# Attention, first expansion and gate folding in an order planned over all engines

## The chip, the cores and the metric

The kernel runs on one core of a Trainium2 chip. The metric is device time in microseconds (us) of one execution. TensorE (PE) multiplies, VectorE (DVE), ScalarE (ACT) and GpSimd (POOL) do the rest, and SyncE (SP) issues the transfers. Each engine runs its own instructions strictly in program order and waits on semaphores for the others.

## What is computed

Inputs are q, k, v of 4 batches, 12 heads, 448 positions and 64 dimensions; a dense expansion 768 to 2048 to 768; and eight experts.

```python
scores = np.where(mask, -1e9, scale * np.matmul(q, k.transpose(0, 1, 3, 2)))   # causal
attn = softmax(scores)
x = np.matmul(attn, v)                       # 1792 tokens x 768
h = x @ w_in                                 # 768 -> 2048, the "first expansion"
g = np.where(h > 0, h, np.exp(np.minimum(h, 0)) - 1)
x = g @ w_out                                # 2048 -> 768
logits = x @ w_gate                          # 8 experts, 224 tokens each, by rank
out = relu(x[chosen] @ w1[e]) @ w2[e]
```

This study is about the lines down to g and about the "gate folding", which computes w_out @ w_gate so that logits come from g directly. The weights w_in and w_out arrive as 8-byte numbers and are converted to 4-byte ones on VectorE.

## The kernel before

**Attention** works on 24 pairs of heads (6 pairs, NP, make one batch). `front(n)` multiplies the scores of pair n, seven tiles of 448 down to 64 columns (tile `sc` in PSUM; for the first six pairs alternately `sc` and `h`, two buffers each). For each tile VectorE masks and takes the row maximum into `s` (L209), ScalarE takes the exponential (L213), VectorE the reciprocals of the sums for three and then four tiles (L220, L221), and GpSimd scales the rows (L228). `back(n)` transposes the scaled tiles on TensorE (tile `tp`, two buffers, L249), copies them to `pt` (L252) and multiplies with v (the second product, tile `pv`, L262). Its result is split into a high part `xh` (ScalarE, L268) and a rest `xl` (VectorE, L269). `att(n)` interleaves `back(n)` with `front(n+1)`.

**The first expansion**, `gemm1(b)`, has 16 feature chunks (MT) for a batch, each the sum over six pairs (KT); one piece (m, c) is three matmuls of 448 columns (L377 to L379, tile `h`, two buffers). For each chunk `split_in` splits a weight tile into `wh` (ScalarE, L361) and `wl` (L362), by a fixed rule on GpSimd for batches 0 to 2 and on VectorE for batch 3. In batch 0 each chunk's weights are first converted by `conv`: a clamp `cv` (L169), a high part `cq` (L174) and a join (L178), all on VectorE, from a staged load `st` of 768 KB.

**The gate folding**, `fold()`, does the same conversion for 16 tiles of w_out, writes each back (`wo_d`), transposes it (L323, six transposes into `tp`), and multiplies with w_gate (L313) and `sel` (L319).

**Order.** `Sched` keeps a model time `now`, advanced by what TensorE's instructions cost. Work of other engines is put in a heap by `after(d, fn)` and written into the program d nanoseconds of model time later; `need(tok)` writes everything up to that work first. Which engine takes an operation is fixed in the code. `drive` takes the next TensorE step from the stream that is furthest behind its weight:

```python
sch.drive((seq(*[att_l(n) for n in range(-1, 6)]), 54000))
for b in range(3):
    g = [(seq(*[att_l(n) for n in range(6 * b + 6, 6 * b + 12)]), 45000), (gemm1(b), 57600)]
```

So the first seven `att_l` run the attention of batch 0 alone, and then `gemm1(b)` runs beside the attention of batch b + 1. The folding starts late in b = 0 and runs through b = 1. `gemm1(3)` follows with the first products of the second expansion, then `gemm2`, the routing and the experts.

## Time and profile before

| | us |
|---|---|
| median of 3 runs | 1049.47 (1047.4 to 1051.67) |
| the profiled execution, its own time | 1051.09 |
| its span, first to last instruction | 1049.3 |
| TensorE busy | 1012.6, 97% of the span |
| VectorE busy | 638.1, 61% |
| ScalarE busy | 469.1, 45% |
| GpSimd busy | 234.4, 22% |

TensorE's busy time is a union of matmuls whose ends are modelled, and a matmul counts as busy from its issue, also while it waits for the one in front. So 97% does not mean that 97% of the span was useful; how much was is found from the distance between starts of matmuls that follow each other without a wait.

### The profile page before, as it was taken

The page shows a single profiled execution, that of the slowest core. Times are in us where ns is not written, and L with a number is a line of the kernel's source. Part 1 is how long each engine was busy: PE and PEld are TensorE (multiplying, and loading weights), DVE is VectorE, ACT ScalarE, POOL GpSimd, SP SyncE. Part 2 cuts the span into 40 slices and gives each one's busy share as a digit, 9 for nine tenths or more (in the row PEclk, how much of TensorE's full clock was granted, in tenths as well). Part 3 has the DMA queues.
Part 4 walks back from the last instruction along what each step waited for, and adds up shares of the span by engine and source line. Part 5 has one row for each costly group of instructions (what it writes and reads, how often), then busy time and mean ns, then how long its engine had stood idle before and what let it go on. Part 6 is the DMA issues. An engine that isn't in the chain of part 4 may idle for free.

```text
span 1049.3 us, 17726 instructions
## 1 busy us (share of the span) xinstructions
PE 1012.6 (97%) x6615; PEld 874.3 (83%) x6615; DVE 638.1 (61%) x1531; ACT 469.1 (45%) x1024; POOL 234.4 (22%) x311
## 2 busy tenths in 40 slices
PE   8799999989999999999999999999999999999997
PEld 4568777667777777888898988999999999999997
DVE  5778866767744333445766566656446766667761
ACT  5565556445455555454212111111245666556651
POOL 4456554334344444000000000000030111101110
PEclk9999999999999999999999999999999999999999
DMA  7545644655622110765333323222166787676800
GB/s 182 141 123 182 208 165 141 224 191 190 210 68 88 63 45 27 256 202 162 106 106 116 121 91 102 72 76 71 67 203 210 242 253 225 210 243 221 261 30 27
DMA packets 110857, 155.32 MB, mean 148 GB/s; under 512 B 29617, under 2 KB 82353, under 8 KB 110770
## 3 DMA queue, kind: packets, MB, share of 16 engines
q1 hardware_dynamic: 108210, 143.17, 43.4%
q0 software_dynamic: 2560, 11.01, 3.5%
q8 instruction: 52, 0.85, 0.3%
q14 instruction: 35, 0.29, 0.1%
HBM read 122.17 MB, written 31.98 MB: 147 GB/s over the span
## 4 chain that ended last, share of the span: by engine, by line
PE 81%; DVE 8%; ACT 3%; DMA 3%; issue 2%; POOL 2%; SPq 0%; POOLq 0%; DVEq 0%; ACTq 0%
PE h L633 9%; PE tp L633 8%; PE h L938 8%; PE h L377 7%; PE sc L990 6%; PE h L379 6%; PE h L378 6%; PE sc L204 5%; PE pv L262 4%; PE h L935 4%; PE tp L249 3%; PE pv L990 3%; PE lg L990 3%; PE lg L772 2%; DMA st<-in_moe_w_out_dram 1%
## 5 line engine op out<-in xcount | busy, mean ns | idle before, releaser
L377 PE MATMUL h<-xh,wh 128*128 128x448 f32 x384 | 170.8, 445 | 0.0
L509 DVE TENSOR_TENSOR wl<-wr,wh 128x768 fp32r<-128x768 f32 x144 | 135.4, 952 | 17.5 <-ACT wh L508 17.2
L379 PE MATMUL h<-xh,wl 128*128 128x448 f32 x384 | 140.9, 367 | 0.0
L378 PE MATMUL h<-xl,wh 128*128 128x448 f32 x384 | 140.7, 366 | 0.0
L213 ACT ACTIVATE s<-s,sm 128x448 f32<-128x448 f32 (+6 forms) x168 | 84.9, 506 | 105.5 <-DVE sm L209 104.8
L508 ACT CAST wh<-wr 128x768 fp32r<-128x768 f32 x144 | 118.2, 829 | 29.9 <-PE lg L990 23.4
L938 PE MATMUL h<-xt,wh 128*128 128x448 f32 x384 | 119.2, 374 | 0.0
L228 POOL TENSOR_SCALAR s<-s,sm 128x448 f32<-128x448 f32 (+6 forms) x168 | 90.2, 554 | 116.2 <-DVE sm L221 105.1
L362 POOL TENSOR_TENSOR wl<-wr,wh 128x768 fp32r<-128x768 f32 x48 | 90.2, 1880 | 106.4 <-ACT wh L361 100.7
L643 ACT COPY x<-h 128x384 f32<-128x384 f32 x14 | 6.7, 480 | 230.5 <-PE h L633 230.5
L204 PE MATMUL sc<-kT,qz 128*128 128x192 f32 (+6 forms) x300 | 92.5, 400 | 5.4 <-DVE sm L209 4.3
L209 DVE CUSTOM_DVE_ANT_0 s<-sc,mask 128x448 f32<-128x448 f32 (+6 forms) x150 | 62.1, 420 | 57.1 <-PE sc L204 51.0
L394 DVE SCALAR_TENSOR_TENSOR g<-e,h 128x448 f32<-128x448 f32 x64 | 39.6, 619 | 88.2 <-ACT e L391 88.1
L935 PE MATMUL h<-xt,wl 128*128 128x224 f32 x384 | 92.2, 267 | 0.0
L377 PEld LDWEIGHTS h<-xh,wh 128*128 128x128 f32 x384 | 72.5, 189 | 17.6 <-issue 9.7
L633 PE MATMUL h<-wh,gh 128*128 128x384 f32 x224 | 81.2, 363 | 0.0
L378 PEld LDWEIGHTS h<-xl,wh 128*128 128x128 f32 x384 | 72.9, 190 | 9.4 <-issue 3.2
L379 PEld LDWEIGHTS h<-xh,wl 128*128 128x128 f32 x384 | 72.4, 188 | 6.7 <-POOL wl L362 0.6
L633 PE MATMUL h<-wl,gh 128*128 128x384 f32 x224 | 77.4, 345 | 0.0
L633 PE MATMUL h<-wh,gl 128*128 128x384 f32 x224 | 76.6, 342 | 0.0
L633 PE MATMUL tp<-wh,gl 128*128 128x384 f32 x224 | 75.4, 336 | 0.0
L633 PE MATMUL tp<-wl,gh 128*128 128x384 f32 x224 | 75.3, 336 | 0.0
(209 smaller groups left out, 2127.7 us busy)
## 6 DMA issues: line engine op xcount, KB each, us to landing
wr<-in_moe_w_dram SPq DMA_DIRECT2D x128, 384.0 KB, 3.8
gT_d<-g SPq DMA_DIRECT2D x64, 224.0 KB, 1.9
gr<-gT_d SPq DMA_DIRECT2D x28, 512.0 KB, 4.0
st<-in_moe_w_in_dram SPq DMA_DIRECT2D x16, 767.6 KB, 4.6
st<-in_moe_w_out_dram SPq DMA_DIRECT2D x16, 767.6 KB, 5.0
wo_d<-wo SPq DMA_DIRECT2D x16, 384.0 KB, 3.2
wr<-wo_d SPq DMA_DIRECT2D x16, 384.0 KB, 3.7
qz<-in_q_dram SPq DMA_DIRECT2D x48, 112.0 KB, 3.3
```

The lines of the kernel that those rows point to most:

```text
L204: PE.matmul(p[:, :w], qT[:, i].rearrange("p a c -> p (a c)"), kT[:, :w], start=True, stop=True)
L228: G.tensor_scalar(s[:, :w], s[:, :w], sm[:, 2, i:i + 1], 1.0, op0=OP.mult, op1=OP.mult)
L362: t = after(800, lambda: (V if b == 3 else G).tensor_sub(wl, WIN[m], wh.bitcast(F32)))
L377: PE.matmul(p[:, :S], wh[:, c], xh, start=(c == 0), stop=False)
L378: PE.matmul(p[:, :S], wh[:, c], xl, start=False, stop=False)
L379: PE.matmul(p[:, :S], wl[:, c], xh, start=False, stop=(c == KT - 1))
L508: A.copy(wh, raw)
L509: return wh, wl, after(gap, lambda: e.tensor_sub(wl, raw, wh.bitcast(F32)))
L633: PE.matmul(p[n][:, :384], st[:, mm], wsel[:, 384 * n:384 * n + 384], start=(m == 0 and first), stop=(m == MT - 1 and st is gl))
L935: PE.matmul(p[:, :CAP], wl[:, c], xt[:, c, :CAP], start=False, stop=stop, skip_group_check=True)
L938: PE.matmul(p[:, :2 * CAP], wh[:, c], xt[:, c], start=(c == 0), stop=(c == KT - 1), skip_group_check=True)
L990: PE.matmul(acc[j][n][:HC, :384], ht[:, m, s, j * HC:(j + 1) * HC], wsel[:, 384 * n:384 * n + 384], start=(m == 0 and first), stop=(m == F ...
```

## The change

`Sched` becomes a list scheduler. `job(cost, deps, fn, prio)` takes a cost for each engine that may do the work; `best` picks, among the jobs whose dependencies have an end in the model, the one that can start first (then by priority), on the engine where it ends first; `pop` books that engine. A stream now yields what its next TensorE step waits for, its cost, and the PSUM buffers that it takes; `drive` takes a step only when the model says that it is ready. Conversions get the lowest priority (3). The split `wl` may go to VectorE or GpSimd (batches 0 to 2), the copies of transposed tiles to ScalarE or VectorE. One pair's `front` may run ahead of `back` by up to two pairs. In the first batch scores use `sc` (two buffers) and `lg` (one), which leaves `h` to the expansion: the first two chunks of `gemm1(0)` take piece (0, c) and (1, c) as soon as pair c is done. The three tiles for v become fixed, with one clearing each instead of 24.

```diff
     def __init__(self):
-        self.now, self.heap, self.n = 0.0, [], 0
+        self.now, self.n, self.jobs, self.free, self.rings = 0.0, 0, [], {}, {}
+
+
+    def job(self, cost, deps, fn, prio=0):
+        self.n += 1
+        tok = Tok()
+        self.jobs.append((prio, self.n, cost, list(deps), fn, tok))
+        return tok
...
+    def ended(self):
+        return Tok(self.now + LAT_PE)
...
+    def best(self):
+        top = None
+        for j in self.jobs:
+            prio, n, cost, deps, fn, tok = j
+            r = self.when(deps)
+            if r is not None:
+                e = min(cost, key=lambda e: max(r, self.free.get(e, 0.0)) + cost[e])
+                z = max(r, self.free.get(e, 0.0)), prio, r, n
+                if top is None or z < top[0]:
+                    top = z, j, e
+        return top
...
+    def pop(self, top):
+        z, j, e = top
+        self.jobs.remove(j)
+        end = z[0] + j[2][e]
+        if e is not None:
+            self.free[e] = end
+        j[5].t = end + (LAT if e is not None else 0.0)
+        j[4](e)
...
-    def drive(self, *gens):
-        st = [[g, 0.0, t] for g, t in gens]
-        while st:
...
+    def drive(self, *streams, until=lambda: False):
+        st = [[[g if isinstance(g, list) else [g, ((), 0.0, ())] for g in (gs if isinstance(gs, tuple) else (gs,))],
...
+        while st and not until():
+            top = self.place(self.now)
+            pick, first, n = None, top and top[0][0], 0
+            for s in st:
+                for g in s[0]:
+                    r = self.ready(g)
+                    if r is None:
+                        continue
+                    if r <= self.now + 60.0:
+                        z, n = s[1] / s[2], n + 1
+                        if pick is None or z < pick[0]:
+                            pick = z, s, g, r
+                        break
+                    first = r if first is None else min(first, r)
+            if pick is None:
+                self.now = max(self.now, first)
+                continue
...
+            self.now = max(self.now, r)
+            self.place(self.now)
+            self.now += g[1][1]
+            s[1] += g[1][1]
...
-                c = next(s[0])
-                s[1] += abs(c)
-                self.tick(max(c, 0))
...
+    def load64(i):
+        if i < 2 * MT:
+            STG[i] = wf.tile([128, DM * 8], U8, name="st")
+            LD[i] = Tok(sch.now + 6500.0)
+            src = w_in[i] if i < MT else w_out[(i - MT) * 128:(i - MT + 1) * 128]
+            SP.dma_start(STG[i][:, :DM * 8 - 3], src.bitcast(U8)[:, 3:])
+
...
+        def join(_):
+            V.scalar_tensor_tensor(dst.bitcast(I32), tl["x"], 5, tl["d"], op0=OP.logical_shift_right, op1=OP.bitwise_or)
+            load64(i + 2)
+
+        t = sch.job({V: 640.0}, [lambda: LD.get(i), lambda: JOIN.get(i - 1)], clamp, 3)
+        t = sch.job({V: 1250.0}, [t], high, 3)
+        JOIN[i] = sch.job({V: 1030.0}, [t], join, 3)
...
+        yield [lambda: DONE.get(n - 2)], 0.0
+        if n + 2 < NB * NP:
+            load_qk(n + 2)
+        if n + 1 < NB * NP:
+            load_v(n + 1)
+        for fn in EARLY.get(n, ()):
+            fn()
         qT, kT = qz[n % 3], KN.pop(n)
         sm = at.tile([128, 3, 8], F32, name="sm", bufs=3)
...
+            nm, nb = ("lg", 1) if n < NP and i in (5, 2) else ("sc", 2)
+            yield [], max(1.68 * w, 222.0), ((nm, nb),)
...
+            def ev(e, p=p, i=ii[0], nb=nb, ni=ni):
+                (V.tensor_copy if e is V else A.copy)(
...
+            w = 128 * nb * ni
+            tk.append(sch.job({A: 0.82 * w + 60, V: 1.04 * w + 90}, [sch.ended()], ev))
...
-            conv_in(m + 2, m + 4)
-        need(WTOK[m])
+            conv_in(m + 2)
         wh = wk.tile([128, KT, 128], F32R, name="wh")
         wl = wk.tile([128, KT, 128], F32R, name="wl")
-        A.copy(wh, WIN[m])
-        t = after(800, lambda: (V if b == 3 else G).tensor_sub(wl, WIN[m], wh.bitcast(F32)))
-        sp[m] = wh, wl, t
+        t1 = sch.job({A: 790.0}, [JOIN[m]], lambda _: A.copy(wh, WIN[m]), 1)
+        t2 = sch.job({V: 930.0} if b == 3 else {V: 930.0, G: 1850.0}, [t1],
+                     lambda e: e.tensor_sub(wl, WIN[m], wh.bitcast(F32)), 1)
+        sp[b, m] = wh, wl, t1, t2
...
-
-        for m in range(MT):
-            wh, wl, tok = sp.pop(m)
-            need(tok)
-            p = ps.tile([128, 512], F32, name="h")
-            for c in range(KT):
-                (t1, xh), (t2, xl) = XH[b * NP + c], XL[b * NP + c]
...
-                yield 567
-                if c == 0:
-                    split_in(b, m + 1)
...
+        P = {}
+        order = [(m, c) for m in range(MT) for c in range(KT)]
+        if b == 0:
+
+            order[:2 * KT] = [(m, c) for c in range(KT) for m in range(2)]
+        for m, c in order:
+            n = b * NP + c
+            yield [lambda: XL[n][0] if n in XL else None, lambda: sp[b, m][3] if (b, m) in sp else None], 609.0, (
+                (("h", 2),) if c == 0 else ())
...
+            split_in(b, m + 2)
...
-    sch.drive((seq(*[att_l(n) for n in range(-1, 6)]), 54000))
-    for b in range(3):
-        g = [(seq(*[att_l(n) for n in range(6 * b + 6, 6 * b + 12)]), 45000), (gemm1(b), 57600)]
-        if b == 0:
-            fd = fold()
-            g.append((seq(wait(85000), one(fd)), 105000))
-        if b == 1:
-            g.append((fd, 18 * 6080))
-        sch.drive(*g)
...
+    EARLY = {1: [lambda: conv_in(0)], 2: [lambda: conv_in(1), lambda: split_in(0, 0)], 3: [lambda: split_in(0, 1)],
+             4: [consts_gate]}
+    stream = lambda g: [g, ((), 0.0, ())]
+    att = stream(seq(*[back(n) for n in range(NB * NP)])), stream(seq(*[front(n) for n in range(NB * NP)]))
+    gem = stream(seq(*[gemm1(b) for b in range(3)]))
+    sch.now = 6000.0
+    sch.drive((att, 1.0e9), (gem, 1.0), until=lambda: NP - 1 in XL)
+    sch.drive((att, 132000), (gem, 182600), (fold(), 1.0e9))
...
-    sch.drive((gemm1(3), 57600), (split_out(), 48000), (logits0(), 45000), (seq(wait(50000), pre()), 51000))
+    sch.drive((gemm1(3), 62000), (split_out(), 48000), (logits0(), 45000), (seq(wait(50000), pre()), 51000))
```

What this makes of the order is shown at three places. The names are those of the code; numbers behind s, qz and vn are buffers.

The first place is VectorE at the end of pair 0's scores, with what each instruction waits for. Before:

```order
L209 ISA s_99,sm<-h,mask 128x128 [waits PE_49]
L209 ISA sm 128x1
L209 ISA s_97,sm<-sc,mask 128x64 [waits PE_49]
L209 ISA sm 128x1
L220 TENSOR_SCALAR sm<-sm 128x3 [waits Activation_49]
L221 RECIPROCAL sm<-sm 128x3 [waits DVE_49]
L209 ISA s_110,sm<-sc,mask 128x448 [waits PE_49]
L209 ISA sm 128x1
```

In the change:

```order
L304 ISA s_99,sm<-sc,mask 128x128 [waits PE_49]
L304 ISA sm 128x1
L261 TENSOR_SCALAR cv<-st 128x768 [waits DMAHW0_49]
L318 TENSOR_SCALAR sm<-sm 128x3 [waits Activation_49]
L319 RECIPROCAL sm<-sm 128x3 [waits DVE_49]
L304 ISA s_97,sm<-sc,mask 128x64 [waits PE_49]
L304 ISA sm 128x1
L304 ISA s_110,sm<-sc,mask 128x448 [waits PE_49]
```

The clamp of the first weight tile, which waits for a transfer, now stands ahead of pair 0's first reciprocals.

The second place is TensorE between the second products of two early pairs (of pairs 0 and 1 before, then of the change):

```order
L204 MATMUL sc<-kT,qz_95 128x192
L204 MATMUL h<-kT,qz_95 128x128
L204 MATMUL sc<-kT,qz_95 128x64
L204 MATMUL sc<-kT,qz_96 128x448
L249 MATMUL tp<-ident,s_110 128x128 x4
L249 MATMUL tp<-ident,s_108 128x128 x3
L249 MATMUL tp<-ident,s_106 128x128 x3
L204 MATMUL h<-kT,qz_96 128x384
L249 MATMUL tp<-ident,s_102 128x2x64 x2
L249 MATMUL tp<-ident,s_104 128x2x64 x2
L249 MATMUL tp<-ident,s_98 128x2x64
L249 MATMUL tp<-ident,s_100 128x2x64
```

```order
L341 MATMUL tp<-ident,s_110 128x128 x4
L341 MATMUL tp<-ident,s_108 128x128 x3
L300 MATMUL sc<-kT,qz_96 128x448
L341 MATMUL tp<-ident,s_106 128x128 x3
L341 MATMUL tp<-ident,s_102 128x2x64 x2
L341 MATMUL tp<-ident,s_104 128x2x64 x2
L300 MATMUL lg<-kT,qz_96 128x384
L341 MATMUL tp<-ident,s_98 128x2x64
L341 MATMUL tp<-ident,s_100 128x2x64
L300 MATMUL sc<-kT,qz_96 128x320
L467 MATMUL h<-xh,wh 128x448
L468 MATMUL h<-xl,wh 128x448
```

The transposes of pair 1 now begin right behind the product of pair 0, since its scores were all written ahead of it, and the first piece of the expansion stands among them.

The third place is VectorE in the middle of the folding. Before:

```order
L169 TENSOR_SCALAR cv<-st 128x768
L209 ISA s_106,sm<-sc,mask 128x320
L209 ISA sm 128x1
L174 ISA cq,dummy<-st,cv 128x768
L174 ISA dummy 128x1
L220 TENSOR_SCALAR sm<-sm 128x3
L221 RECIPROCAL sm<-sm 128x3
L209 ISA s_104,sm<-sc,mask 128x256
L209 ISA sm 128x1
L178 SCALAR_TENSOR_TENSOR wo<-st,cq 128x768
L394 SCALAR_TENSOR_TENSOR g<-e,h 128x448
L325 COPY woT<-tp 128x384
```

In the change:

```order
L361 TENSOR_TENSOR xl<-pv,xh 128x448
L446 TENSOR_TENSOR wl<-wr,wh 128x768
L261 TENSOR_SCALAR cv<-st 128x768
L484 SCALAR_TENSOR_TENSOR g<-e,h 128x448
L419 COPY wp<-tp 128x8
L265 ISA cq,dummy<-st,cv 128x768
L265 ISA dummy 128x1
L268 SCALAR_TENSOR_TENSOR wo<-st,cq 128x768
L304 ISA s_103,sm<-sc,mask 128x256
L304 ISA sm 128x1
L446 TENSOR_TENSOR wl<-wr,wh 128x768
L304 ISA s_101,sm<-sc,mask 128x192
```

The weight rests wl now stand on VectorE between two conversions. Of the 64 wl of the first expansion VectorE does 58 in the change and 16 before, GpSimd 6 and 48. Between the xl of pair 10 and that of pair 14 VectorE has 14 conversions in the change and 11 before. From the 77th matmul of the second expansion on, the order of TensorE is the same as before but for a shift of two routing steps.

## Rows read from the trace of the kernel before

**Rows 1.** Timeline of TensorE beside the expansion: start us, us, what, count.
```profile
150.46 0.36 PE L377 MATMUL h<-xh,wh 128*128 128x448 f32 x1
...
151.07 0.70 PE L204 MATMUL sc<-kT,qz 128*128 128x320 f32 x2
```

**Rows 2.** Timeline of TensorE, first pairs; in brackets idle before and its releaser.
```profile
1.19 4.45 PE L446 MATMUL pv<-warm 128*128 128x512 bf16 x10 [1.19 <-DVE warm L443]
...
12.97 1.11 PE L249 MATMUL tp<-ident,s 128*128 128x128 f32 x7 [0.47 <-POOL s L228]
...
14.75 0.81 PE L204 MATMUL h<-kT,qz 128*128 128x384 f32 x2
15.40 0.82 PE L249 MATMUL tp<-ident,s 128*128 128x128 f32 x6
16.05 0.70 PE L204 MATMUL sc<-kT,qz 128*128 128x320 f32 x2
```

**Rows 3.** The chain that ended last: start us, us, what; second products of pairs 5, 10, 17, 23.
```profile
63.20 1.88 PE pv L262 x16
...
154.05 1.88 PE pv L262 x16
...
310.15 1.88 PE pv L262 x16
...
414.11 1.88 PE pv L262 x16
```

**Rows 4.** Timeline of TensorE in the folding.
```profile
187.67 0.42 PE L313 MATMUL tp<-woT,wg 128*32 128x128 f32 x6
```

**Rows 5.** Stretches: length, busy us of PE, PEld, DVE, ACT, POOL, clock, DMA share, GB/s.
```profile
63.20:154.05 90.85, 87.70 (x482) 70.61 (x483) 71.25 (x175) 52.05 (x133) 50.53 (x54) 1.00 0.53 167
154.05:310.15 156.10, 147.35 (x986) 111.94 (x988) 102.52 (x262) 80.45 (x213) 61.06 (x74) 0.99 0.54 179
310.15:414.11 103.96, 102.16 (x587) 80.76 (x588) 40.47 (x136) 57.90 (x147) 48.31 (x62) 1.00 0.18 57
...
191.90:264.00 72.10, 68.42 (x476) 51.52 (x475) 52.14 (x126) 36.13 (x97) 29.27 (x32) 0.98 0.63 204
```

**Rows 6.** Tile st, loads of the first 14 us: count, ns, first and last start us.
```profile
L152 SPq DMA_DIRECT2D st<-in_moe_w_in_dram x2: 583/584/585, 5.7 to 9.4; - x2
...
DMA to landing us min/median/max: 7.8/7.8/7.8
```

**Rows 7.** Timeline of VectorE, pair 0.
```profile
11.88 0.17 DVE L221 RECIPROCAL sm<-sm 128x3 f32<-128x3 f32 x1
```

**Rows 8.** VectorE groups by form, 0 to 500 us: count, busy us, mean ns, idle before.
```profile
L174 DVE CUSTOM_DVE_ANT_0 cq<-st,cv 128x768 int32<-128x768 int8 x32 | 44.6, 1394 | 0.1
...
L394 DVE SCALAR_TENSOR_TENSOR g<-e,h 128x448 f32<-128x448 f32 x64 | 39.6, 619 | 88.2 <-ACT e L391 88.1
L169 DVE TENSOR_SCALAR cv<-st 128x768 bf16<-128x768 int8 x32 | 21.2, 662 | 10.5 <-DMA st<-in_moe_w_out_dram 10.5
...
L178 DVE SCALAR_TENSOR_TENSOR wo<-st,cq 128x768 int32<-128x768 int32 x16 | 16.8, 1050 | 0.1
...
L362 DVE TENSOR_TENSOR wl<-wr,wh 128x768 fp32r<-128x768 f32 x16 | 15.2, 952 | 0.3
...
L209 DVE CUSTOM_DVE_ANT_0 s<-sc,mask 128x448 f32<-128x448 f32 x24 | 14.8, 616 | 4.3 <-PE sc L204 4.3
...
L209 DVE CUSTOM_DVE_ANT_0 s<-sc,mask 128x64 f32<-128x64 f32 x24 | 5.3, 221 | 4.4 <-PE sc L204 3.8 <-POOL vn L145 0.4
```

**Rows 9.** Tile st, first 60 us: ns min/median/max.
```profile
L174 DVE CUSTOM_DVE_ANT_0 cq<-st,cv x3: 1115/1115/1117, 31.0 to 50.6; 128x768 int32<-128x768 int8 x3
```

**Rows 10.** GpSimd groups by form, 0 to 500 us.
```profile
L362 POOL TENSOR_TENSOR wl<-wr,wh 128x768 fp32r<-128x768 f32 x48 | 90.2, 1880 | 106.4 <-ACT wh L361 100.7 <-PE tp L323 5.4
L228 POOL TENSOR_SCALAR s<-s,sm 128x448 f32<-128x448 f32 x24 | 18.1, 756 | 61.9 <-DVE sm L221 52.9 <-ACT s L213 9.0
```

**Rows 11.** Waits of VectorE, 150 to 300 us: us in total, times, longest.
```profile
DVE cv L169 <- DMA st<-in_moe_w_out_dram: 10.5, 5, 4.4
```

More of the change, by code (lines that the diff above doesn't have):

```diff
@@ L34, with __init__, ring, hold @@
 MASK = -8.0e9
+LAT_PE, LAT = 300.0, 60.0
+class Tok:
+    def __init__(self, t=None):
+        self.t = t
 class Sched:
     def __init__(self):
[L42 to L53 removed]
+        self.now, self.n, self.jobs, self.free, self.rings = 0.0, 0, [], {}, {}
[4 more added lines that the diff above has]
+        return tok
+    def after(self, d, fn):
+        return self.job({None: 0.0}, [Tok(self.now + d)], lambda e: fn())
+    def ended(self):
+        return Tok(self.now + LAT_PE)
+    def ring(self, name, n):
+        r = self.rings.setdefault(name, [])
+        return r[-n] if len(r) >= n else []
+    def hold(self, name, *toks):
+        self.rings.setdefault(name, []).append(list(toks))
+    def when(self, deps):
+        r = 0.0
+        for d in deps:
+            d = d() if callable(d) else d
+            if d is None or d.t is None:
+                return None
+            r = max(r, d.t)
+        return r
+    def best(self):
[17 more added lines that the diff above has]
+        j[4](e)
+    def place(self, t):
+        while True:
+            top = self.best()
+            if top is None or top[0][0] > t:
+                return top
+            self.pop(top)
@@ new lines, in ready @@
+    def ready(self, g):
+        deps, _, rings = g[1]
+        return self.when(list(deps) + [d for n, k in rings for d in self.ring(n, k)])
+    def drive(self, *streams, until=lambda: False):
+        st = [[[g if isinstance(g, list) else [g, ((), 0.0, ())] for g in (gs if isinstance(gs, tuple) else (gs,))],
+               0.0, w] for gs, w in streams]
+        while st and not until():
[15 more added lines that the diff above has]
+                continue
+            _, s, g, r = pick
+            self.now = max(self.now, r)
+            self.place(self.now)
+            self.now += g[1][1]
+            s[1] += g[1][1]
+            try:
+                c = next(g[0])
+                g[1] = (c + ((),))[:3] if isinstance(c, tuple) else ((), 0.0, ())
+                if not isinstance(c, tuple):
+                    s[1] += abs(c)
+                    self.now += max(c, 0)
+                    if c < 0 and n == 1 and first is not None:
+                        self.now = max(self.now, first)
@@ L128, in body @@
     PB = [[at.tile([128, 128 * ((i + 2) // 2)], F32, name=f"s{i}{k}", bufs=1) for k in range(2)] for i in range(NQ)]
-    KN, VN, WIN, STG = {}, {}, {}, {}
+    VT = [at.tile([128, 4, 2, D], F32, name=f"vn{i}", bufs=1) for i in range(3)]
+    KN, WIN = {}, {}
     def load_qk(n):
@@ new lines, in gemm1 @@
+        order = [(m, c) for m in range(MT) for c in range(KT)]
[5 more added lines that the diff above has]
+                (("h", 2),) if c == 0 else ())
+            GPOS[0] = max(GPOS[0], b * MT + m)
+            if c == 0:
+                P[m] = ps.tile([128, 512], F32, name="h")
+            p = P[m]
+            wh, wl = sp[b, m][:2]
+            xh, xl = XH[n][1], XL[n][1]
+            PE.matmul(p[:, :S], wh[:, c], xh, start=(c == 0), stop=False)
+            PE.matmul(p[:, :S], wh[:, c], xl, start=False, stop=False)
+            PE.matmul(p[:, :S], wl[:, c], xh, start=False, stop=(c == KT - 1))
+            if c == 1 and b == NB - 1:
+                load_wo(m)
+            if c == 3 and LATE:
+                yield from late()
+            if c < KT - 1:
+                continue
+            split_in(b, m + 2)
@@ L403, in gemm1 @@
                 gs = []
+        G1[b] = sch.ended()
     LATE, L_TOK = [], []
@@ L449, in body @@
     load_v(0)
-    load64_in(0)
+    load64(0)
+    load64(1)
     for t in qz:
```

272 lines of the change are left out of this document (99 added, 173 removed).

## The prediction

> **What bounds the kernel now.** I read the chain of waits first. It runs almost wholly over TensorE, so time is won only where TensorE has nothing to do or waits. Its busy share can't show that, so I price its work by the distance of starts. One piece of the expansion, three matmuls, holds it 0.61 us: the first of three starts at 150.46 and the next other work at 151.07 [rows 1]. A score tile of 384 columns holds it 0.65 us (14.75 to 15.40), and six transposes as long (15.40 to 16.05) [rows 2]; so a pair's seven tiles with 1792 columns cost 3.0 us and its 16 transposes 1.74. The second product takes 1.88 us [rows 3]. A pair is 6.6 us of TensorE. One folding tile is six transposes, 0.65, and small products of some 0.4 [rows 4]; a group of logits is taken as 1 us, half a second product.
>
> Then I set the starts of second products in the chain [rows 3] against the work that the program has between them, counted in its order.
>
> - To 63.20 us (pair 5): 4.4 us of warming matmuls [rows 2] and 6 pairs and 4 score tiles, less the product that follows, 40.1: 44.5 of work, 18.7 lost.
> - 63.20 to 154.05 (pairs 6 to 10): 5 pairs 33.1, 83 pieces 50.6: 83.7 of 90.9, 7.2 lost.
> - 154.05 to 310.15 (pairs 11 to 17, with the folding): 7 pairs 46.3, 106 pieces 64.7, 16 folding tiles 17, three logit groups 3: 131 of 156.1, 25 lost.
> - 310.15 to 414.11: 6 pairs less four score tiles 37.3, 92 pieces 56.1, four logit groups 4: 97.4 of 104.0, 6.6 lost. Behind it nothing worth a term.
>
> So some 57 us are lost before 414 us, and the reader is to see where: in the head and in the folding. VectorE is the busiest helper: 71.25 of 90.85 us beside batch 0's expansion, 102.52 of 156.10 in the folding, 52.14 of 72.10 in its densest part, but only 40.47 of 103.96 behind it [rows 5].
>
> **The change, part by part.** TensorE's work is the same, so each term is a part of these losses. The terms go against the profiled execution, 1051.09 us (its span is 1049.3); the median of before is 1.6 lower.
>
> *Head.* Two things pull apart. Against: the clamp of the first weights now stands on VectorE ahead of pair 0's reciprocals. Its load is issued at 5.7 us and lands 7.8 us later [rows 6], at 13.5; the planner assumed 6.5 us. The reciprocals ended at 12.05 [rows 7] and the transposes came 0.9 later, at 12.97 [rows 2]. In the change: 13.5, clamp 0.7 [rows 8], reciprocals 0.4, then 0.9: 15.5, 2.5 us later. TensorE meanwhile does two more score tiles of pair 1 (1.2 us), so 1.3 are lost. Behind the first transposes come the others, each pair of them waiting for a copy out of the two tp buffers on a ScalarE and a VectorE that have pair 1's tiles to do as well: 5.5 us by my walk through both orders, then the product, which ends at 22.9. Whether the second weight load, now issued right behind the first, delays it, no row shows: at most by its own length, 768 KB at 203 GB/s [rows 5], 3.8 us, and the lower bound below takes that in. The Trainium skill (DMA: Bandwidth & Descriptors, Queues, rings and completion order) says that on each DMA engine descriptors are consumed in ring order; by that there is no such delay.
> For: pair 1's scores are written by then, its transposes follow at once, and pieces of the expansion fill gaps. From 22.9 I go pair by pair with the larger of TensorE's and VectorE's work. Pairs 1, 3, 4, 5 are TensorE's: 6.2, 6.7, 8.7, 7.0 with small waits. Pair 2 is VectorE's: up to its xl the change has 4 clamps, 4 high parts, 3 joins and 2 wl where before has 2, 1, 1 and 0, 8.6 us more by [rows 8], the high part at the 1.115 that it took this early [rows 9]; less what backlog pair 1 leaves room for, it takes 10.4. The sum, 39.0, puts the start of pair 5's product at 60.0 us instead of 63.2, with 3.4 us more work done (five pieces and a small tile): 6.6 gained. I take 5, since a walk by hand leaves out small waits; bounds 2 and 8.
>
> *Pairs 6 to 10.* VectorE's work is close to TensorE's here in both orders (it ran 78% of the time and 7.2 us were lost). I take 1; bounds -2 and 3.
>
> *Folding.* The planner spreads it over 0.88 chunks a tile, which is denser than before, and gives VectorE the wl. Between pair 10 and pair 14 VectorE has, at the means of [rows 8]: 14 conversions (0.66 + 1.39 + 1.05) 43.5; 10 wl 9.5; 11 g 6.8; 30 row maxima, a pair's seven being 2.9 by the ends 0.62 and 0.22, 12.6; and some 12 of xl, reciprocals and copies (three kinds that this sum takes as before): 84 us. TensorE has 81 of work there (4 pairs, 64 pieces, 12 to 13 folding tiles, one logit group). With both full, neither can wait for the other without loss. I take 93 us, that is VectorE at 90%, nearer to its work than to its 78% beside batch 0: 12 lost, and 5 in the three pairs behind, where two conversions are left: 17 instead of 25, a gain of 8. Bounds: VectorE at 97% (87 us), a gain of 14; VectorE at 78%, the share of pairs 6 to 10, 108 us, a loss of 7. The new order has two merits here: a step is taken only when its inputs are due, so that transposes no longer stand in front of work that could run, and copies may go to ScalarE.
>
> *GpSimd.* It keeps the row scalings and 6 wl. That cost is hidden: its two groups had 62 and 106 us of idle time before them [rows 10]. But wl costs VectorE 0.95 us [rows 8] each, 42 of them 40 us over batches 0 to 2; only in the folding is there no slack for them, and there they are in the sum. One row gives part of it back: the high part took 1.115 us in the first 60 us [rows 9], when GpSimd had no wl, and 1.394 in the mean [rows 8]. 14 times 0.28 is 4 us less for VectorE in the dense part. The Trainium skill (SBUF — State Buffer, Who interferes with whom) says that a VectorE instruction with two SBUF inputs contends with a GpSimd instruction that reads SBUF; the two rows agree. But by the same rule the wl on VectorE now meets the row scalings: at most 10 times 0.76 [rows 10], and some 2 us if GpSimd scales rows a fifth of the time. I leave both out of the sum; they lie within its bounds.
>
> *Behind 310 us, and gemm1(3) on.* VectorE has slack; 0 taken, bounds 0 and 2. TensorE's later order is unchanged.
>
> Sum: 5 + 1 + 8 + 0 = 14; 1051.09 - 14 = 1037.1 for a profiled execution, 1035.5 for the median. All bounds together: 27 better and 7 worse.
>
> **The rivals.**
>
> *The planned order works better (A).* Head 8, pairs 6 to 10 3, folding 14, rest 2: 27 less, 1022.5. For it: the head's and folding's losses are order losses, and the high part gets cheaper. Against: VectorE has as much to do as TensorE.
>
> *VectorE becomes the bound of the folding and eats the gain (B).* At 78%, folding costs 7, with head 5 and 1: 1051 less 0 or so, about 1050; no change. For it: the share in the densest part before was 72% [rows 5]. The Trainium skill (Perfetto Trace Analysis, Optimizing Scalar/DVE Operations) advises to move work away from a saturated VectorE, which is what the new wl do not. By that rule this rival is the likely one; here the 78% row gives its time. Against: before, TensorE's own waits kept VectorE short of work.
>
> *Slower (C): a clamp waits for its staged load and holds VectorE's whole queue.* In the folding VectorE waited 10.5 us in 5 of the 16 clamps [rows 11], 2.1 us each. In the change 14 clamps come in 93 us; a load is issued by the join two tiles earlier and can stand behind SP's waits for TensorE. If all 14 wait 2.1 us, VectorE being full, 29 us come on top: 1064.5. It is slower by 0.5% from 19 us of such waits, 1.4 per clamp. Against: a load has nearly two conversions, 13 us, to land, and the slow ones at the start took 7.8 [rows 6].
>
> **How the numbers follow.** The forecast, a gain of 6 to 20, has a chance of 0.66; A 0.13, B 0.13, C 0.08, which sum to 1. The number is the forecast's, 1035.5. Its own range is 1029 to 1044. The range reaches to A and B, past their times by what their own bounds are worth, and leaves out C and the far edge of A: 1020 to 1049. A measurement of this kernel tells about 0.5%, 5 us, from no change. Faster by more than that are the forecast and A, 0.79; within it is B, 0.13; slower is C, 0.08.
>
> **What would show it.** Right: the start of pair 5's second product at 59 to 62 us with five pieces behind it; first transposes at 15 to 16 us, with VectorE's clamp ahead of them ending at 14 to 15; VectorE busy 85% or more between pairs 10 and 14, which take 88 to 98 us; the high part nearer 1.15 us; GpSimd's busy time down by some 80 us. Wrong: first transposes as early as 13, or pair 2 without a VectorE queue (head); pairs 10 to 14 over 105 us (B, and C if the waits at cv name a DMA); a stretch behind 414 us that is longer than before, which no term covers.

## The result, and the profile after

The changed kernel takes 1036.29 us (median of 4 runs, 1034.43 to 1040.33) beside 1049.99 us before: a ratio of 0.9877, 95% interval 0.9839 to 0.9914, or 1.2% faster. The profiled run is the longest of the four, 1040.33 us, span 1038.5. Its engines:

```profile
PE 1008.8 (97%) x6615; PEld 875.1 (84%) x6615; DVE 642.4 (62%) x1540; ACT 489.5 (47%) x1057; POOL 153.7 (15%) x248
```

The chain that ended last, for [rows 3] (start us, us, what: second products of pairs 0, 10, 17, 23), and the timeline's row of pair 5, which the chain leaves out:

```profile
22.57 1.95 PE pv L354 x16
...
145.77 1.88 PE pv L354 x16
...
295.18 1.88 PE pv L354 x16
...
396.50 1.95 PE pv L354 x16
...
62.62 1.24 PE L354 MATMUL pv<-pt,vn 128*64 128x448 f32 x6
```

The stretches between them, for [rows 5], the folding also up to pair 14, and two short ones (length, busy us of PE, PEld, DVE, ACT, POOL, granted clock, DMA share, GB/s):

```profile
62.62:145.70 83.08, 77.08 (x433) 61.96 (x433) 63.13 (x158) 51.92 (x130) 29.91 (x40) 1.00 0.51 168
145.70:238.10 92.40, 89.69 (x635) 69.37 (x634) 69.25 (x180) 57.03 (x148) 20.73 (x30) 1.00 0.79 241
145.70:295.10 149.40, 146.09 (x995) 112.72 (x994) 100.74 (x268) 89.69 (x231) 30.60 (x50) 1.00 0.61 187
295.10:396.50 101.40, 100.48 (x578) 78.56 (x578) 49.69 (x149) 63.21 (x155) 20.04 (x42) 1.00 0.18 57
...
13.90:20.70 6.80, 5.65 (x21) 4.82 (x22) 4.88 (x23) 4.22 (x15) 3.56 (x8) 0.50 0.56 135
...
474.70:478.10 3.40, 3.40 (x11) 3.00 (x10) 0.68 (x1) 0.45 (x1) 0.00 (x0) 0.50 0.59 183
```

I set each start against the work ahead of it, counted and priced as in the prediction. "Lost" is what a stretch takes beyond that. What TensorE loses, before and after: up to pair 5 18.7 and 14.8 us, pairs 6 to 10 7.2 and 9.3, pairs 11 to 17 25.1 and 16.0, pairs 18 to 23 6.4 and 5.2. From there to the last matmul of gemm1(3) it is 3.6 worse, and in the rest of the program 2.3 better. The sum is 10.8 us, the difference of the two spans. The folding gives most. Of its 9.1 us, 5.4 are idle time of TensorE, 8.8 us before [rows 5] and 3.3 after; more comes from a stretch of 3.4 us at half clock that before had at 191 us. The longest single wait there before was for row scalings, whose four-column sum on VectorE took 1.45 us, instead of 0.16, beside a wl on GpSimd (TensorE, GpSimd, VectorE):

```profile
229.41 0.52 PE L249 MATMUL tp<-ident,s 128*128 128x128 f32 x3 [2.87 <-POOL s L228]
...
224.66 2.05 POOL L362 TENSOR_TENSOR wl<-wr,wh 128x768 fp32r<-128x768 f32 x1 [7.33 <-ACT wh L361]
...
225.29 1.45 DVE L220 TENSOR_SCALAR sm<-sm 128x4 f32<-128x4 f32 x1 [0.25 <-ACT s L213]
```

Two places lose, pairs 6 to 10 and the tail, and the head gains less than it could. What stands there is in the timelines of VectorE (first row) and TensorE (in brackets: idle before, and who ended it):

```profile
14.03 0.56 DVE L261 TENSOR_SCALAR cv<-st 128x768 bf16<-128x768 int8 x1 [3.94 <-DMA st<-in_moe_w_in_dram]
...
15.05 1.43 PE L300 MATMUL sc<-kT,qz 128*128 128x320 f32 x2 [3.22 <-DVE sm L304]
16.28 1.06 PE L341 MATMUL tp<-ident,s 128*128 128x128 f32 x4
...
76.56 1.95 PE L354 MATMUL pv<-pt,vn 128*64 128x448 f32 x16 [2.17 <-ACT e L481]
...
110.09 0.66 PE L341 MATMUL tp<-ident,s 128*128 128x128 f32 x4 [1.29 <-POOL s L325]
...
131.93 0.66 PE L341 MATMUL tp<-ident,s 128*128 128x128 f32 x4 [1.73 <-POOL s L325]
...
472.68 1.02 PE L517 MATMUL pv<-sel,e 128*128 128x8 f32 x8 [1.12 <-DVE e L508]
```

The clamp waits for its load as foreseen; new is that the clock granted to TensorE then falls to half for 6.8 us (320 columns take 1.43 us instead of 0.81). The tail has a wait of 1.12 us that before had not, and half clock behind it. Between pairs 5 and 10 TensorE has three long waits, and each has a wl on GpSimd beside it. For the first, at 76.56, the view names ScalarE's e, but that had ended at 76.00; the product also needs a copy into pt that VectorE ended at 76.46, behind a high part that took 2.55 us beside a wl. The second, at 110.09, is for row scalings whose four-column sum took 1.24 us, instead of 0.16, beside a wl. The third is for row scalings too. Here are the first and the third, each on GpSimd and on VectorE:

```profile
73.49 1.81 POOL L446 TENSOR_TENSOR wl<-wr,wh 128x768 fp32r<-128x768 f32 x1 [1.60 <-ACT wh L444]
...
73.57 2.55 DVE L265 CUSTOM_DVE_ANT_0 cq<-st,cv 128x768 int32<-128x768 int8 x1
...
76.05 0.41 DVE L344 COPY pt<-tp 128x256 f32<-128x256 f32 x1
...
128.48 1.84 POOL L446 TENSOR_TENSOR wl<-wr,wh 128x768 fp32r<-128x768 f32 x1 [12.09 <-ACT wh L444]
130.30 3.90 POOL L325 TENSOR_SCALAR s<-s,sm 128x256 f32<-128x256 f32 x7
...
128.67 2.46 DVE L265 CUSTOM_DVE_ANT_0 cq<-st,cv 128x768 int32<-128x768 int8 x1
```

At 130.30 the scalings stand behind one of the six wl that are left on GpSimd (five of them in these pairs), and the high part beside that wl takes 2.46 us on VectorE. All 32 high parts (count, busy us, mean ns, idle before):

```profile
L265 DVE CUSTOM_DVE_ANT_0 cq<-st,cv 128x768 int32<-128x768 int8 x32 | 34.9, 1091 | 0.6
```

The mean is 1.09 us, where it was 1.39 [rows 8].

### The profile page after: what moved, and what is told of

Same layout as the page of the kernel before. It is cut to its first block, busy times and chain, and to the rows that moved or that the text cites. A ratio compares the mean times of both kernels' runs of the same rounds, so it can differ in the third digit from the quotient of the medians.

```text
span 1038.5 us, 17732 instructions
## 1 busy us (share of the span) xinstructions
PE 1008.8 (97%) x6615; PEld 875.1 (84%) x6615; DVE 642.4 (62%) x1540; ACT 489.5 (47%) x1057; POOL 153.7 (15%) x248
## 3 DMA queue, kind: packets, MB, share of 16 engines
q1 hardware_dynamic: 108210, 143.17, 43.5%
## 4 chain that ended last, share of the span: by engine, by line
PE 82%; DVE 7%; DMA 3%; ACT 2%; issue 2%; POOL 2%; SPq 0%; POOLq 0%; DVEq 0%; ACTq 0%
PE h L703 9%; PE tp L703 8%; PE h L1008 8%; PE h L467 7%; PE h L468 7%; PE sc L1060 6%; PE h L469 6%; PE sc L300 5%; PE h L1005 4%; PE pv L354 4%; PE tp L341 3%; PE pv L1060 3%; PE lg L1060 3%; PE lg L842 2%; PE lg L430 1%
## 5 line engine op out<-in xcount | busy, mean ns | idle before, releaser
L579 DVE TENSOR_TENSOR wl<-wr,wh 128x768 fp32r<-128x768 f32 x144 | 135.4, 953 | 18.5 <-ACT wh L578 18.0
L578 ACT CAST wh<-wr 128x768 fp32r<-128x768 f32 x144 | 118.2, 828 | 29.2 <-PE lg L1060 23.4
L325 POOL TENSOR_SCALAR s<-s,sm 128x448 f32<-128x448 f32 (+6 forms) x168 | 92.9, 570 | 259.5 <-DVE sm L319 168.4
L308 ACT ACTIVATE s<-s,sm 128x448 f32<-128x448 f32 (+6 forms) x168 | 84.7, 505 | 58.3 <-DVE sm L304 57.2
L446 DVE TENSOR_TENSOR wl<-wr,wh 128x768 fp32r<-128x768 f32 x58 | 55.9, 964 | 68.9 <-ACT wh L444 67.7
L300 PE MATMUL sc<-kT,qz 128*128 128x448 f32 (+6 forms) x312 | 93.6, 397 | 4.6 <-DVE sm L304 3.7
L444 ACT CAST wh<-wr 128x768 fp32r<-128x768 f32 x64 | 53.4, 834 | 82.6 <-PE h L468 79.9
```

Source lines behind the costliest of these rows:

```text
L300: PE.matmul(p[:, :w], qT[:, i].rearrange("p a c -> p (a c)"), kT[:, :w], start=True, stop=True)
L308: A.activation(s[:, :w], s[:, :w], AF.Exp, bias=sm[:, 0, i:i + 1], scale=-1.0, accum_out=sm[:, 1, i:i + 1])
L325: G.tensor_scalar(s, s, sm[:, 2, u:u + 1], 1.0, op0=OP.mult, op1=OP.mult)
L578: A.copy(wh, raw)
L579: return wh, wl, after(gap, lambda: e.tensor_sub(wl, raw, wh.bitcast(F32)))
```

## Experiments

All were timed against the kernel before on the same chip, in five rounds; "lost" is meant as above.

**The changed kernel again.** No edit. 

> The changed kernel once more, unedited, as the yardstick of the three that run beside it: median 1034 to 1038. Two readings of its first profile are put to the test of a second: that the 3.2 us wait ahead of pair 0's transposes, with the granted clock at half behind it, and the 1.1 us wait for logits0's copy near 471 us are of the program and come again (theory: both within 0.5 us), or were of that one execution (rival: one of them is gone and the span is 2 to 3 us shorter). Second products of pairs 5, 10, 17, 23 at 62.6, 145.7, 295.1, 396.5 within 0.7 us.

1035.35 us, ratio 0.986 (0.9831 to 0.989). The profiled span is 8 us shorter than the first, 1030.5. The load landed earlier:

```profile
12.58 0.56 DVE L261 TENSOR_SCALAR cv<-st 128x768 bf16<-128x768 int8 x1 [2.65 <-DMA st<-in_moe_w_in_dram]
...
13.60 0.81 PE L300 MATMUL sc<-kT,qz 128*128 128x320 f32 x2 [1.93 <-DVE sm L304]
...
59.14:142.30 83.16, 77.17 (x434) 62.00 (x433) 63.16 (x158) 51.95 (x130) 29.97 (x40) 1.00 0.53 168
142.30:231.94 89.64, 89.07 (x634) 69.42 (x633) 69.93 (x180) 57.17 (x148) 18.87 (x30) 1.00 0.83 247
```

TensorE waits 1.93 us instead of 3.22 and its clock stays at full: pair 5's product comes at 59.14, 3.5 us earlier. The wait in the tail is the same 1.12 us, without half clock. So both waits are the program's, but the first is as long as the landing of the load makes it, and the half clock behind them comes in some executions only. Neither expectation held: the first wait differs by 1.3 us, not 0.5, none of the two is gone, and the four second products come 3.4 to 6.1 us earlier. Pairs 6 to 10 repeat to 0.1 us, and their waits with them; pairs 11 to 17 take 146.7 us instead of 149.4, so a single profile of the folding is good to some 3 us. The reader should look at the last row: from pair 10 to pair 14 TensorE is busy 89.07 of 89.64 us.

**The clamp placed by the real landing.** 

> The planner is told when the first two weight loads really land (14.5 and 16.5 us instead of 6.5), so the clamp no longer stands ahead of pair 0's reciprocals. Theory (the head pays for the clamp's wait, and for the half clock behind it): first transposes at 12.5 to 13.5 us instead of 16.3, no stretch of half clock before 21 us, pair 5's second product at 59 to 61 us instead of 62.6 with two more pieces (1.2 us) done, total 3 to 5 us less than the changed kernel. Rival (VectorE's work for the first weights bounds the head from pair 2 on, so an earlier start is only waited away later): pair 5's product within 1 us of 62.6 and the total within 1 us.

```diff
-    load64(1)
+    load64(1); LD.update({0: Tok(14500.0), 1: Tok(16500.0)})
```

1035.23 us, no different. The head did gain, and more than expected: first transposes at 11.57, pair 5's product at 55.64 with two more pieces. But pairs 6 to 10 lose 13.1 instead of 9.4:

```profile
55.64:147.19 91.55, 83.72 (x458) 66.81 (x457) 71.10 (x176) 55.64 (x141) 29.86 (x41) 0.98 0.56 172
...
66.04 2.29 PE L300 MATMUL sc<-kT,qz 128*128 128x320 f32 x4 [2.21 <-DVE sm L304]
```

A wait of 2.21 us for VectorE's row maxima, half clock with it, and 1.6 us of the same kind at 120 us. The row maximum stood behind a wl on VectorE that took 1.84 us beside one on GpSimd. On the total the rival was right; its place for the loss, the head from pair 2 on, was not, since that part took 40.1 us from pair 0's product to pair 5's with two more pieces done, as long as without them.

**The turning of logits0 later.** 

> The turning of logits0 stands five pieces later in TensorE's order, all else is the same. Theory (the tail's loss is the 1.1 us wait for the copy on VectorE and the half clock behind it): no wait there, no half clock from 474.7 to 478.1, the last matmul of gemm1(3) some 2.5 us earlier, total 2 to 3 us less. Rival (the clock's fall has another cause, or the wait comes back at the next gate): 1.1 us or less.

```diff
-        L_TOK.append(after(1500, turn_logits))
+        L_TOK.append(after(4000 if b == 0 else 1500, turn_logits))
```

Logits0 are the logits of the first batch: VectorE copies them, and TensorE turns them by products with `sel`. In the program the turning stands four pieces later, behind nine pieces instead of five. 1034.31 us (ratio 0.9845, 0.982 to 0.9871), 1.0 less, which the intervals don't tell from none. The wait is gone, no half clock follows, and from pair 23 to the last matmul of gemm1(3) it takes 81.5 us instead of 84.7 in the first profile and 83.1 in the second. By its size the total goes with the rival, the 1.1 us of the wait alone; the clock's share comes only in some executions.

**No growth of the first chunks.** 

> The growth of the first two chunks is undone: no piece of the expansion until pair 5 is through, then chunk by chunk; planner, clamps and copies stay. Theory (the five pieces ahead of pair 5's product fill gaps of TensorE, as the sum for the head had it: 3.0 us of work for nothing): pair 5's product at 61.5 to 62.6 us, no more than 1 us earlier, the five pieces paid for later, total 2 to 3 us more than the changed kernel. Rival (the head is bound by VectorE, which has the same work either way, and pieces missing there are made up in gaps behind it): pair 10's product within 1 us of 145.7 and the total within 1 us.

```diff
-            order[:2 * KT] = [(m, c) for c in range(KT) for m in range(2)]
+            pass
-    sch.drive((att, 1.0e9), (gem, 1.0), until=lambda: NP - 1 in XL)
+    sch.drive((att, 1.0e9), until=lambda: NP - 1 in XL)
```

1034.8 us (ratio 0.9829, 0.9798 to 0.9859): the rival by the total; pair 10's product, at 144.35, is 1.4 us earlier, just beyond its 1 us. The five pieces do fill gaps (pairs 1 to 5 lose 6.4 us without them, 4.3 with), but pairs 6 to 10 then lose 5.8 instead of 9.4. The planner put three wl on GpSimd in these pairs instead of five, and TensorE's waits for row scalings there fall from 3.2 to 0.7 us, so the edit changed more than the growth. As it stands the growth is worth nothing that can be measured.

**More VectorE work in the folding.** 

> Each conversion of the folding issues its clamp twice (16 instructions more on VectorE, 0.56 us each, 9 us in all, 8 of them between the second products of pairs 10 and 14); the planner knows nothing of it, so the order is the changed kernel's. The prediction's step (VectorE, at 84 us of work, is what the stretch from pair 10 to pair 14 hangs on): the stretch grows by some 7 us from 89.6 to 92.4, the total by 5 to 8 us. Theory after the result (VectorE was busy only 70 us there and TensorE is the bound): VectorE's busy time up by 8, the stretch 92 us or less, the total within 2 us of 1035.

```diff
-            V.tensor_scalar(tl["c"], tl["y"], -56.0, 56.0, op0=OP.max, op1=OP.min)
+            [V.tensor_scalar(tl["c"], tl["y"], -56.0, 56.0, op0=OP.max, op1=OP.min) for _ in range(2 if i >= MT else 1)]
```

1039.53 us, 4.2 more; its ratio, 0.9902 (0.9881 to 0.9923), just overlaps that of the unedited kernel, so the size is rough. Pair 10 to pair 14, and two rows of TensorE in it:

```profile
143.04:237.74 94.70, 90.19 (x634) 69.03 (x633) 76.69 (x194) 57.09 (x148) 20.70 (x30) 1.00 0.81 235
...
150.50 0.84 PE L406 MATMUL tp<-ident,wo 128*128 128x128 f32 x6 [1.02 <-DVE wo L268]
...
175.06 0.55 PE L406 MATMUL tp<-ident,wo 128*128 128x128 f32 x3 [1.20 <-DVE wo L268]
```

VectorE is busy 6.8 us more, 81% of the stretch, which is 5.1 us longer than 89.64 and 2.3 longer than the first profile's 92.40. The late turning, which has the same program up to there, gives a third value, 90.78. My theory after the result falls: VectorE is not full and yet the work is not free, because TensorE now waits for the joins behind the second clamps, 2.2 us in all, where the three profiles without second clamps have 0.2 to 0.8.

**The same, and the planner knows it.** 

> As the run with the clamp twice (8 us more on VectorE between pairs 10 and 14, which cost that stretch 5.1 and the total 4.2), but the planner is told that a clamp of the folding takes 1.2 us instead of 0.64. Theory (VectorE has room in the stretch; what the second clamp cost was lateness, since everything in VectorE's queue came later than the order of TensorE assumed): pair 10 to pair 14 at 91 us or less with VectorE's busy time still near 77, the total within 2 us of 1035.3. Rival (VectorE's work itself is what the stretch hangs on, the prediction's step): 94 us or more again, total 1038 to 1041.

```diff
-        t = sch.job({V: 640.0}, [lambda: LD.get(i), lambda: JOIN.get(i - 1)], clamp, 3)
+        t = sch.job({V: 1200.0 if i >= MT else 640.0}, [lambda: LD.get(i), lambda: JOIN.get(i - 1)], clamp, 3)
```

```profile
146.75:239.42 92.67, 89.53 (x633) 69.50 (x632) 76.23 (x189) 56.71 (x147) 23.86 (x30) 1.00 0.79 233
```

92.67 us lies between the two expectations, with VectorE as busy as in the run ahead. Pairs 11 to 17 take 149.1 us; the unedited kernel 149.4 and 146.7 in its two profiles, the unknowing planner 152.3. TensorE's waits for joins are gone, and it waits 1.5 us for copies of ScalarE and 1.1 for row scalings instead. That points to lateness as the price, but does not show it: one program's profiles differ by 2.8 us in this stretch, and the planner also moved two more wl to GpSimd, eight instead of six. The total, 1039.24 (0.9888, 0.9871 to 0.9906), is that of the unknowing planner and stands with the rival; its interval overlaps the unedited kernel's too, and in this profile half clock also followed the wait near 76 us. The case is not settled.

**No wl on GpSimd, and all wl on GpSimd.** 

> GpSimd gets no wl at all: the planner's second engine for it is struck out, so the six of batches 0 to 2 that went there go to VectorE (six times 1.0 us). Theory (a wl on GpSimd costs more than its own time: the row scalings stand behind it, and VectorE's two-input instructions beside it are stretched, a high part from 0.96 to 2.46 us): the waits of 1.45 and 1.90 us of transposes for GpSimd between pairs 5 and 10 are gone, no high part beyond 1.3 us in that stretch, pair 10's product 2 to 4 us earlier than in the unedited kernel after the same pair 0, total 1031 to 1034. Rival (VectorE is short of time in this stretch): pair 10 no earlier, total within 1 us of 1035.

> All 42 wl of batches 0 to 2 go to GpSimd, as in the kernel before, under the new planner. Theory A (the gain is one of order; VectorE has room for wl and they are better there): slower than the changed kernel by 2 to 8 us, through row scalings that stand behind a wl and stretched high parts, but still faster than before. Theory B, the prediction's (VectorE is the scarce engine of the folding, its ten wl there cost 9.5 us): pair 10 to pair 14 shorter by 3 us or more than 89.6, total 1032 or less. Rival C (moving wl off GpSimd was the whole gain): back to 1047 to 1051.

```diff
-        t2 = sch.job({V: 930.0} if b == 3 else {V: 930.0, G: 1850.0}, [t1],
+        t2 = sch.job({V: 930.0}, [t1],
```
```diff
+        t2 = sch.job({V: 930.0} if b == 3 else {G: 1850.0}, [t1],
```

All means 48 wl; the 42 of the expectation are those that leave VectorE. With none 1031.73 us (ratio 0.9823, 0.9803 to 0.9843), with six 1035.35, with 48 1040.24 (0.9915, 0.9898 to 0.9933). First none, the high part between pairs 5 and 10 (ns min/median/max), then all, TensorE, GpSimd and VectorE near 72 us and the folding up to pair 17:

```profile
L265 DVE CUSTOM_DVE_ANT_0 cq<-st,cv x12: 928/955/1079, 73.0 to 143.2; 128x768 int32<-128x768 int8 x12
```

```profile
75.16 2.29 PE L300 MATMUL sc<-kT,qz 128*128 128x320 f32 x4 [3.26 <-DVE sm L304]
...
70.00 4.30 POOL L446 TENSOR_TENSOR wl<-wr,wh 128x768 fp32r<-128x768 f32 x2 [4.91 <-ACT wh L444]
...
70.24 2.39 DVE L268 SCALAR_TENSOR_TENSOR wr<-st,cq 128x768 int32<-128x768 int32 x1
72.55 1.76 DVE L318 TENSOR_SCALAR sm<-sm 128x4 f32<-128x4 f32 x1
...
155.67:296.05 140.38, 139.29 (x964) 107.00 (x963) 87.25 (x227) 86.03 (x224) 60.39 (x66) 1.00 0.60 184
```

Without wl there, the two long waits for row scalings are gone, the wait ahead of a second product falls from 2.17 to 0.60 us, and pairs 6 to 10 lose 6.3 instead of 9.4. The gain is not where the theory put it: pair 10's product comes 124.1 us behind pair 0's and not earlier than the 123.1 and 123.2 of the unedited kernel, but with 4 us more of TensorE's work done ahead of it. With all of them there, beside two wl of 4.30 us together a join takes 2.39 us instead of 0.95 and the four-column sum ahead of the reciprocals 1.76 instead of 0.16; TensorE waits 3.26 us behind both. Pairs 6 to 10 lose 14.3, with half clock from 74.0 to 80.9. In the folding VectorE is busy 87 us instead of 101 and nothing comes of it: pairs 11 to 17 lose 13.7 beside 13.4 (they are shorter by the work that stands elsewhere). Theory A. B's sign came, pair 10 to pair 14 in 86.37 us, but with 3.7 us less of TensorE's work in it, and the total denies B; C falls. The Trainium skill (SBUF — State Buffer, Who interferes with whom) says that a VectorE instruction with two SBUF inputs contends with a GpSimd instruction that reads SBUF; the stretched high part and join agree. The four-column sum has one SBUF input, which that sentence does not cover.

**Fixed engines for the copies.** 

> The copies of P transposed go to fixed engines as in the kernel before (the second and the fourth of five to VectorE, the others to ScalarE), the planner is left the rest. Theory (where a copy goes is worth little, since neither engine is full): total within 2 us of 1035.3, pairs 11 to 17 within 2 us of 146.7 for the same work. Rival (the free choice of engine is a main part of the folding's gain): 4 us or more slower, with waits of TensorE for tp copies on one of the two engines.

```diff
-            tk.append(sch.job({A: 0.82 * w + 60, V: 1.04 * w + 90}, [sch.ended()], ev))
+            tk.append(sch.job({V: 1.04 * w + 90} if ii[0] in (5, 2) else {A: 0.82 * w + 60}, [sch.ended()], ev))
```

1040.92 us (ratio 0.9919, 0.9898 to 0.9939), 5.6 more: the rival. VectorE now has 48 of the 120 copies, where the planner had given it 24. Not all of the 5.6 is the copies': with them fixed the planner put ten wl on GpSimd instead of six. Up to pair 10 it loses as much as the unedited kernel's second profile (20.9 and 20.8 us); pairs 11 to 17 lose 3.7 more and pairs 18 to 23 2.3 more, with waits as this one:

```profile
272.49 1.95 PE L354 MATMUL pv<-pt,vn 128*64 128x448 f32 x16 [0.99 <-ACT pt L344]
```

**The edits that helped, together.** 

> Two edits together: no wl on GpSimd (alone 1031.7) and the turning of logits0 five pieces later (alone 1.0 less). Theory: the two are apart in time and add up: 1030 to 1031.5, no wait ahead of the turning, pair 10 and pair 17 as with the first edit alone (84.1 and 142.8 us long). Rival (the tail's wait costs only by the half clock that follows in some executions): no less than 1031.5.

> The two edits and the right landing times of the first two weight loads. Theory (the head's wait for the load is 4 us of TensorE that nothing behind it needs to give back; alone it did not shorten the kernel because the half clock at 66 us and two waits of 2.4 and 1.8 us for score tiles ate it, all in the order that happened to follow): pair 0's product near 15.6, pair 5's near 55.6 us with seven pieces, total 1027 to 1029.5. Rival (what the head gains VectorE takes back between pairs 5 and 10, whatever the order): pairs 5 to 10 lose 11 us or more against their work instead of 6.3, total within 1 us of the run with the two edits.

> The two edits (no wl on GpSimd, turning of logits0 later), and the folding spread thinner: a tile every 1.2 chunks from chunk 10 on instead of every 0.88 from chunk 12 on; VectorE's conversions are spread with it. The program up to pair 10 is the same and from pair 10 to pair 23 has the same work in both. Theory (at the changed kernel's own load TensorE is the bound of the folding, busy 84.6 of 85.7 us from pair 10 to pair 14, so there is nothing for VectorE to give back): pair 10 to pair 23 within 1 us of the 244.1 us of the run with the two edits, total within 1 us of 1030.8. Rival (the density of VectorE's work still costs there, the prediction's step): 3 us or more shorter, total 1028 or less.

The edits are those above, and for the last one also:

```diff
-    FOLD0, FOLDN = 12, 0.88
+    FOLD0, FOLDN = 10, 1.2
```

No wl on GpSimd and the late turning: 1030.8 us (ratio 0.9813, 0.9795 to 0.983), as the sum of both has it, though 0.9 us is within the noise. With the landing times as well 1029.76 (0.9807, 0.9794 to 0.982): pair 5's product at 55.24, and pairs 6 to 10 lose 9.6 us instead of 6.4. The rival's mechanism again, short of its 11; the total, 1.0 less, lies between both expectations. With the folding spread thinner 1028.7 (0.9786, 0.9765 to 0.9806), from pair 10 to pair 23:

```profile
141.82:385.96 244.14, 241.51 (x1555) 188.27 (x1554) 149.23 (x404) 152.00 (x384) 48.23 (x89) 1.00 0.43 134
```

```profile
147.72:391.71 243.99, 241.28 (x1555) 188.21 (x1554) 146.43 (x402) 153.15 (x386) 46.03 (x88) 1.00 0.43 135
```

First the two edits, then with the spread: the same. The spread gives the stretch nothing, as expected; its total, 2.1 us lower, is between both expectations, can't be derived from the stretch, and its interval overlaps that of the two edits. All three beat both kernels, by about 2% the one before.

## Why the prediction was right, and where its working was not

**The number** held: a gain of 14 was forecast, 13.7 came, and 15.5 beside before in the second measurement. Its terms did not all hold, and that the sum did is in part luck: against the one profile of before the two profiles of the change gain 10.8 and 18.8 us, the difference being the landing of a load, the half clock and the folding, and the 3 us missed at pairs 6 to 10 stand beside terms that came out up to 4 us larger.

**Head** (5 taken; 4.0 measured, 0.6 us of start and 3.4 of extra work; 7.5 in the second profile). Right: the clamp ahead of the reciprocals, the order of waits, pair 2 as the slow one (10.4, measured 9.7), and the time from pair 0's product to pair 5's (39.0, measured 40.1 in both profiles). Mis-sized: "1.3 are lost" while the clamp waits. TensorE stood still for 3.2 us, and the half clock behind that was in no term: the first transposes came at 16.28 instead of 15.5, and pair 0's product, forecast to end at 22.9, ended at 24.5. In the execution without half clock, where the load landed 1.4 us earlier, it ended at 21.0, and pair 5 starts at 59.14, just inside the step's 59 to 62. So the 5 lies between two executions, and what decides most of it is the landing, which took 5.4 to 8.9 us in the 13 profiles of the new order; the prediction had 7.8.

**Pairs 6 to 10** (1 taken, -2.1 measured). The step "I take 1" failed in its sign. The prediction looked at VectorE's load alone. What stood there was GpSimd: five of its six wl run in these pairs, ahead of row scalings and beside stretched instructions of VectorE, which the step "That cost is hidden" priced at nothing from GpSimd's idle time. With no wl on GpSimd this stretch loses 6.3 us, 0.9 less than the 7.2 of before, which is the 1 that was taken.

**Folding** (8 taken, 9.1 and in the second profile 11.7 measured). The time from pair 10 to pair 14 was forecast at 93 us and is 92.40 and 89.64, but the step "VectorE at 90%" failed, so the time is right by luck. VectorE is busy 69 to 70 us, 75 to 78%, not 84; its groups there, among them

```profile
L265 DVE CUSTOM_DVE_ANT_0 cq<-st,cv 128x768 int32<-128x768 int8 x14 | 13.6, 969 | 0.2
L268 DVE SCALAR_TENSOR_TENSOR wo<-st,cq 128x768 int32<-128x768 int32 x14 | 13.4, 958 | 0.1
...
L446 DVE TENSOR_TENSOR wl<-wr,wh 128x768 fp32r<-128x768 f32 x10 | 9.7, 972 | 3.5 <-ACT wh L444 2.5 <-PE sc L300 1.0
L261 DVE TENSOR_SCALAR cv<-st 128x768 bf16<-128x768 int8 x14 | 7.8, 554 | 7.3 <-DMA st<-in_moe_w_out_dram 7.3
```

add up to 80.5 us of durations, and 69.25 of busy time, since each instruction starts before the one ahead of it has ended. That is two errors. A sum of mean durations counts this overlap, 11 us, as work. And the means were those of before, where wl ran on GpSimd: they priced the conversions (34.8 us) at 43.5. With all wl back on GpSimd the new order has the old prices in this stretch:

```profile
L265 DVE CUSTOM_DVE_ANT_0 cq<-st,cv 128x768 int32<-128x768 int8 x13 | 16.4, 1260 | 0.2
L268 DVE SCALAR_TENSOR_TENSOR wo<-st,cq 128x768 int32<-128x768 int32 x14 | 15.2, 1084 | 0.1
L261 DVE TENSOR_SCALAR cv<-st 128x768 bf16<-128x768 int8 x13 | 10.3, 796 | 0.5 <-DMA st<-in_moe_w_out_dram 0.4
```

A conversion is 3.14 us there (3.10 in the prediction) and 2.48 with wl on VectorE, 9.2 us less for 14; so the ten wl, 9.7 us, cost VectorE almost nothing. What bounds the stretch is TensorE, idle for 0.6 of 89.64 us in the second profile: in the folding neither the 14 us less on VectorE with all wl on GpSimd nor the thinner spread lowered what TensorE loses. Part of what I called lost is a folding tile that costs more than my 1.05 us: by the distances of starts the 13 tiles take some 18 us in the second profile, an estimate of 1.4 each. Still VectorE is no spare engine: 7 us more, unknown to the planner, cost some 4 in the total.

**GpSimd** is down by 80.7 us as forecast (234.4 to 153.7). The contention that the prediction noted and left out of the sum belonged in it: wl moved back to GpSimd cost 4.9 us, the last six moved away bring 3.6. Fixed copies cost 5.6, with four more wl on GpSimd among it. So these two free choices carry a large part of the gain, but they overlap and need not add up. What the order alone brings was not run by itself, nor were the fixed tiles for v, the `lg` tiles in the head, or `front` running ahead.

**Behind** (0 taken): 1.2 better up to pair 23, then 3.6 worse. That loss was the one kind which the prediction named as covered by no term: 1.1 us of wait and the half clock behind it, and 0.8 us that I can't place. The rest of the program is 2.3 us better, and 1.6 to 2.5 in the other profiles, with TensorE's order the same but for the shift of two routing steps; its cause is open.

**The rivals.** C's waits exist, 7.3 us in the first row of the clamps above, 0.5 a clamp instead of 2.1, but TensorE waits only 0.2 to 0.8 us for joins. B's danger is real, since more work on VectorE there does cost time, but its price was wrong: with VectorE at 75 to 78% the stretch takes 90 to 92 us, not 108. A's 1022.5 was not reached, with 1028.7 the best of the experiments.

## What to carry to other kernels

Before moving work onto an engine, subtract the overlap: busy time in a window, not a sum of mean durations, is what that engine has used. A stretch in which TensorE is at 99% can still be lengthened by more work on an engine at 78%: here TensorE then waited 2.2 us for joins that came late, so look at when a result is due and not at load alone. How much of that price is lateness stayed open. And an instruction on GpSimd costs what stands behind it and what it stretches on VectorE, even where GpSimd idles most of the time; taking it away gave VectorE back, in cheaper conversions, nearly all that it took over.

## What was not expected of the hardware

TensorE's clock is one thing that makes executions differ. In the head it stayed at 2.4 GHz after waits of 1.26, 1.93 and 1.96 us and was at 1.2 GHz, for 3.4 or 6.8 us, during or after waits of 2.70 to 4.49 us in eight profiles. The length of the wait alone does not decide it: the kernel before has a wait of 2.87 us at 229 us at full clock, and 3.4 us of half clock behind one of 1.42 us at 189. In the tail the same wait of 1.1 us was followed by half clock in four profiles and not in five; and of five profiles with the same wait of 2.2 us near 75 us, one had half clock behind it. And one and the same first load, issued at 5.7 us, landed 5.4 to 8.9 us later.
